# Stores of converted weight tiles issued by GpSimd instead of the sync engine

## The chip, the cores and the metric

The kernel runs on one NeuronCore of one Trainium2 chip. The metric is the device time of one execution in microseconds (us), taken as the median of several runs. Engine names in the text: PE is TensorE, DVE is VectorE, ACT is ScalarE, POOL is GpSimd, SP is the sync engine, whose queue issues transfers and computes nothing. "Issued by" an engine means that the instruction that starts a transfer stands in that engine's instruction stream and waits there for its conditions.

## The reference

Three layers follow one another: attention over a window of 64 positions (batch 4, 8 heads, 576 positions, head size 64), a gated feed-forward layer (512 to 1536 to 512) and a second one (512 to 2048 to 512), over 2304 tokens.

```python
scores = scale * np.matmul(q, k.transpose(0, 1, 3, 2))
mask = (rel >= 0) & (rel < 64)                  # rel: query position - key position
attn = softmax(np.where(mask, scores, -1e9))
x = np.matmul(attn, v)                          # [2304 tokens, 512]
g = x @ w_gate
x = (g * (1.0 / (1.0 + np.exp(-g))) * (x @ w_val)) @ w_out
h = x @ w_in
out = (h * np.clip(h + 3.0, 0.0, 6.0) / 6.0) @ w_out2
```

All weights arrive as 64-bit numbers and are made into pairs of 32-bit numbers on the chip.

## The kernel before, in words

**Weights.** The 68 raw weight tiles lie in DRAM as 128 x 512 numbers of 64 bits. The generator `w_ops` (called through `pump`) converts them, a few instructions at each call: ACT makes a float of the high word (L129) and scales the low word in place (L134), DVE clips, shifts and merges (L148, L151, L186, L192), ACT writes the rounded half `t[:, 0]` (L183) and DVE the remainder `t[:, 1]` (L199). The result is a tile of 128 x 1024 float32, a high and a low part. The 36 tiles of the first feed-forward layer stay in SBUF and are used there; 26 of them are also stored to the DRAM tensors `w1d` by `save_w` (L291), since their space is reused later and they are loaded again for the last blocks. The tiles of the second layer (32 raw ones and 16 sums of them, 48 in all) are written to staging tiles `ws` and stored to `w2d` at once (L205). A staging tile `ws` and a raw tile share the same five buffers (tag "raw"), so that a raw load (L107) can take a buffer only when the store of the `ws` tile that was in it has landed.

**Attention and the first layer.** After a first block of attention (0 to about 46 us), the first layer runs in 512-token blocks 0, 1 and 2, each in 12 steps. A step multiplies by the gate and value weights (L542 to L544), forms the product u, and adds the previous step's u times the output weights to four accumulators (L592 to L594). Between them stand the pieces of one attention group: scores (`scores`, L390), softmax on DVE and ACT, transposes (L452), the copy of the transposed tile out of PSUM (`evac_t`, L460, tile pt), the product with v (`values`, L471) and its copy (`store_x`). The loads of the next group, qk (L374, L377) and v (L382), are issued from SP, as are the raw weights. Step n calls `pump` three times, and from step 6 on it calls `save_w` once.

**Order.** Each engine works through its instructions in one fixed order. In the first block and from block 2 on the order is that of the code (`manual_schedule`). In blocks 0 and 1 a scheduler that models the engines and queues in time chooses the order of every engine's instructions, so a transfer that is issued by another engine can move instructions of all of them.

**Later stages.** The last 768 tokens of the first layer run in a form with fewer products (`wide_chunk`, about 396 to 520 us), and the second layer (`unit`, to the end) in two passes of 8 units, with the weights loaded from `w2d`.

Of the kernel before, what the change touches and what calls it, by code (L numbers as in the profile page):

```python
# [69 lines left out]
def attention_two_ffn(ctx: ExitStack, tc, qk, qq, v, w, out):  # L70
    nc = tc.nc
# [37 lines left out]
    def load_ahead(n):  # L109

        while len(w_loaded) <= n + (4 if len(w_loaded) < NW1 else 3):
            w_loaded.append(len(w_loaded))
            w_load(w_loaded[-1])

    def w_ops():

        held, words = {}, {}

        def begin(n):
            held[n] = cv.tile([128, 512], F32, tag="wf", name="wf", bufs=4)
            if raw_of[n] is not None:
                raw = w_raw.pop(raw_of[n])
                both = raw.bitcast(U32).rearrange("p (n t) -> p n t", t=2)
                words[n] = both[:, :, 0], both[:, :, 1]
                nc.scalar.activation(held[n], words[n][1].bitcast(F32), AF.Abs)  # L129

        def begin_low(n):
            if n in words:
                low = words[n][0]
                nc.scalar.activation(low.bitcast(I32), low, AF.Copy, scale=2.0 ** -29)  # L134

        begin(0)
        yield
        begin_low(0)
        yield
        for n in range(NV + 2):  # L140
            raw_n = raw_of[n] if n < NV else None
            new, sums, old = raw_n is not None, n < NV and raw_n is None, n >= 2
            if n < NV:
                f = held[n]
            if new:
                low, high = words.pop(n)
                u = f.bitcast(U32)
                nc.vector.tensor_scalar(f, f, F64_LOW, F64_HIGH, op0=ALU.max, op1=ALU.min)  # L148
                yield
            if new:  # L150
                nc.vector.tensor_scalar(  # L151
                    u, u, 3, 0x3FFFFFFF, op0=ALU.logical_shift_left, op1=ALU.bitwise_and
                )
                yield
            if sums:
                s0, s1 = f[:, 0:256], f[:, 256:512]
                if raw_of[n - 1] is not None:
                    fa, fb = held[n - 2], held[n - 1]
                    nc.vector.tensor_tensor(out=s0, in0=fb[:, 0:256], in1=fb[:, 256:512], op=ALU.add)
                    yield  # L160
                    nc.vector.tensor_tensor(out=s1, in0=s0, in1=fa[:, 0:256], op=ALU.subtract)
                    yield
                else:
                    fa, fb, fs = keep
                    nc.vector.tensor_tensor(
                        out=s0, in0=fa[:, 0:256], in1=fb[:, 0:256], op=ALU.subtract
                    )
                    yield
                    nc.vector.tensor_tensor(
                        out=s1, in0=fa[:, 256:512], in1=fs[:, 256:512], op=ALU.subtract  # L170
                    )
                    yield
            if n + 1 < NV:
                begin(n + 1)
                yield
            if old:
                if n - 2 < NW1:
                    pool = wp if n - 2 in ring else wq
                    t = pool.tile([128, 2, 512], F32R, tag="w", name="wt")
                else:  # L180
                    t = cv.tile([128, 2, 512], F32R, tag="raw", name="ws", bufs=5)
                o_f = held.pop(n - 2)
                nc.scalar.copy(t[:, 0, :], o_f)  # L183
                yield
            if new:
                nc.vector.scalar_tensor_tensor(  # L186
                    out=u, in0=high, scalar=0xC0000000, in1=u,
                    op0=ALU.bitwise_and, op1=ALU.bitwise_or,
                )
                yield  # L190
                i = f.bitcast(I32)
                nc.vector.tensor_tensor(out=i, in0=i, in1=low.bitcast(I32), op=ALU.add)  # L192
                load_ahead(raw_n)
                yield
            if n + 1 < NV:
                begin_low(n + 1)
                yield
            if old:
                nc.vector.tensor_tensor(  # L199
                    out=t[:, 1, :], in0=o_f, in1=t[:, 0, :].bitcast(F32), op=ALU.subtract  # L200
                )
                if n - 2 < NW1:
                    w_tile[n - 2] = t
                else:
                    nc.sync.dma_start(  # L205
                        out=w2_d[n - 2 - NW1],
                        in_=t.rearrange("p a n -> p (a n)").bitcast(F32),
                    )
                yield
            if sums and raw_of[n - 1] is not None:  # L210
                keep = fa, fb, f

    w_iter = w_ops()

    def pump(k):
# [72 lines left out]
    stream += [(load_w, ("w1o", c), w1_d[3 * c + 2]) for c in range(NC1)]  # L288

    def save_w(n):  # L290
        nc.sync.dma_start(  # L291
            out=w1_d[n], in_=w_tile[n].rearrange("p a n -> p (a n)").bitcast(F32)
        )

# [715 lines left out]
    with ExitStack() as fixed:  # L1010
# [10 lines left out]
        for n, (t, c) in enumerate(steps1):  # L1021
# [50 lines left out]
            if n >= SAVE_FROM and saves:  # L1072
                save_w(saves.pop(0))
# [144 lines left out]
```

## Time and profile before

| What | Value |
|---|---|
| Median of 3 runs (lowest, highest) | 920.91 us (919.66, 922.62) |
| Profiled execution | 920.93 us |
| Its span, first to last instruction | 919.1 us |
| PE busy | 891.6 us (97%), 5088 matmuls |
| DVE busy | 701.7 us (76%) |
| ACT busy | 418.1 us (45%) |
| POOL busy | 2.7 us, 14 instructions |
| DMA packets on the queue q1, SP's | 206.47 MB, 64.6% of 16 engines' time |

Busy time is the time that instructions of the engine were running; register work, waiting and the issuing of transfers do not count. PE's matmuls overlap, and their ends are modelled, so that the starts of neighbouring matmuls say more than their lengths. A row of waits names an instruction that stood still, what released it, how long in total, how many times, and the longest. A row of a transfer is its issue; when its bytes have arrived is its landing.

### The profile page before, as it was taken

What the parts mean: (1) busy time and instruction counts of PE and PEld (TensorE: products, weight loads), DVE (VectorE), ACT (ScalarE), POOL (GpSimd) and SP (SyncE); (2) the same over time, 40 slices, a digit from 0 to 9 for tenths busy, and PEclk for the clock granted to TensorE, in tenths of its full rate; (3) what the DMA queues carried; (4) which work ended last, traced back from release to release, by engine and by line L of the source; (5) the groups of instructions that cost most, each with busy time, mean ns of one, the idle gap of its engine ahead of it and who ended that gap; (6) DMA issues with size and microseconds to landing.
All of it is one profiled execution on the core that took longest, in us unless ns stands there. A gap on an engine that the chain in (4) does not pass through costs nothing.

```text
span 919.1 us, 14495 instructions
## 1 busy us (share of the span) xinstructions
PE 891.6 (97%) x5088; PEld 779.9 (85%) x5088; DVE 701.7 (76%) x1629; ACT 418.1 (45%) x994; POOL 2.7 (0%) x14
## 2 busy tenths in 40 slices
PE   5699999999999999999999999999999999999998
PEld 4487788887777778899999999898989898989896
DVE  7899999988887788698888667667666767565654
ACT  7788987665776766344444432222132222211111
POOL 1000000000000000000000000000000000000000
PEclk9799999999999999999999999999999999999999
DMA  8467997787785978315545479765477565485601
GB/s 325 134 196 237 354 352 258 245 296 273 260 307 171 333 279 296 132 60 194 181 146 168 178 303 359 251 217 192 161 293 294 194 207 203 169 311 198 215 24 69
DMA packets 67608, 207.52 MB, mean 226 GB/s; under 512 B 7248, under 2 KB 14416, under 8 KB 67152
## 3 DMA queue, kind: packets, MB, share of 16 engines
q1 hardware_dynamic: 67392, 206.47, 64.6%
q8 instruction: 40, 0.66, 0.3%
q14 instruction: 32, 0.26, 0.1%
q10 hardware_dynamic: 144, 0.13, 0.0%
HBM read 157.16 MB, written 49.41 MB: 225 GB/s over the span
## 4 chain that ended last, share of the span: by engine, by line
PE 65%; DVE 1%; ACT 1%; issue 0%; ACTq 0%; DVEq 0%
PE acc L891 5%; PE acc L892 5%; PE acc L890 5%; PE v L849 3%; PE v L851 3%; PE v L850 3%; PE g L849 3%; PE g L851 3%; PE g L850 3%; PE acc L593 2%; PE acc L594 2%; PE acc L592 2%; PE d L892 1%; PE c L892 1%; PE d L890 1%; PE c L890 1%
## 5 line engine op out<-in xcount | busy, mean ns | idle before, releaser
L870 ACT CAST gh<-g 128x384 fp32r<-128x384 f32 x96 | 49.3, 514 | 195.8 <-DVE g L861 165.2
L872 DVE TENSOR_TENSOR gl<-g,gh 128x384 fp32r<-128x384 f32 x96 | 53.3, 556 | 45.3 <-ACT gh L870 45.2
L593 PE MATMUL acc<-ul,wt 128*128 128x512 f32 (+1 forms) x216 | 81.6, 378 | 0.5 <-DVE ul L570 0.5
L594 PE MATMUL acc<-uh,wt 128*128 128x512 f32 (+1 forms) x216 | 80.4, 372 | 0.0
L892 PE MATMUL acc<-wt,gl 128*128 128x512 f32 x192 | 75.2, 391 | 0.0
L891 PE MATMUL acc<-wt,gh 128*128 128x512 f32 x192 | 75.1, 391 | 0.0
L890 PE MATMUL acc<-wt,gh 128*128 128x512 f32 x192 | 74.7, 389 | 0.0
L592 PE MATMUL acc<-uh,wt 128*128 128x512 f32 (+1 forms) x216 | 73.3, 373 | 0.2 <-ACT uh L565 0.2
L542 PE MATMUL g<-xh,wt 128*128 128x512 f32 x144 | 59.8, 415 | 3.3 <-ACT xh L331 2.8
L429 ACT ACTIVATE y<-y,s 128x128 f32<-128x128 f32 x144 | 56.2, 393 | 12.2 <-DVE s L423 11.9
L134 ACT ACTIVATE raw<-raw 128x512 int32<-128x512 uint32 x68 | 46.0, 677 | 30.9 <-DMA raw<-w_t 30.7
L542 PE MATMUL v<-xh,wt 128*128 128x512 f32 x144 | 57.3, 398 | 0.5 <-DVE u L585 0.4
L543 PE MATMUL g<-xl,wt 128*128 128x512 f32 x144 | 57.5, 399 | 0.2 <-DVE xl L332 0.2
L849 PE MATMUL v<-xh,wt 128*128 128x384 f32 x168 | 56.7, 338 | 0.4 <-ACT q L936 0.4
L544 PE MATMUL g<-xh,wt 128*128 128x512 f32 x144 | 57.1, 396 | 0.0
L849 PE MATMUL g<-xh,wt 128*128 128x384 f32 x168 | 56.6, 337 | 0.0
L544 PE MATMUL v<-xh,wt 128*128 128x512 f32 x144 | 56.5, 393 | 0.0
L851 PE MATMUL v<-xh,wt 128*128 128x384 f32 x168 | 56.4, 336 | 0.0
L851 PE MATMUL g<-xh,wt 128*128 128x384 f32 x168 | 56.4, 336 | 0.0
L850 PE MATMUL v<-xl,wt 128*128 128x384 f32 x168 | 56.3, 335 | 0.0
L850 PE MATMUL g<-xl,wt 128*128 128x384 f32 x168 | 56.3, 335 | 0.0
L543 PE MATMUL v<-xl,wt 128*128 128x512 f32 x144 | 56.2, 390 | 0.0
(214 smaller groups left out, 2274.1 us busy)
## 6 DMA issues: line engine op xcount, KB each, us to landing
wt<-w2d SPq DMA_DIRECT2D x144, 512.0 KB, 4.9
raw<-w_t SPq DMA_DIRECT2D x68, 512.0 KB, 5.0
w2d<-ws SPq DMA_DIRECT2D x48, 512.0 KB, 4.6
wt<-w1d SPq DMA_DIRECT2D x33, 512.0 KB, 4.4
w1d<-wt SPq DMA_DIRECT2D x26, 512.0 KB, 5.3
v<-v_t SPq DMA_DIRECT2D x36, 256.0 KB, 4.5
qk<-qk_t SPq DMA_DIRECT2D x21, 416.0 KB, 5.1
x_out<-ob SPq DMA_DIRECT2D x17, 256.0 KB, 2.1
```

Source lines behind the costliest of these rows:

```text
L542: nc.tensor.matmul(dst, wt[:, 0, col], hi, start=kc == 0, stop=False)
L543: nc.tensor.matmul(dst, wt[:, 0, col], lo, start=False, stop=False)
L544: nc.tensor.matmul(dst, wt[:, 1, col], hi, start=False, stop=kc == KC - 1)
L592: nc.tensor.matmul(a, wt[:, 0, col], hi, start=c == 0, stop=False)
L593: nc.tensor.matmul(a, wt[:, 0, col], lo, start=False, stop=False)
L594: nc.tensor.matmul(a, wt[:, 1, col], hi, start=False, stop=c == NC1 - 1)
L849: nc.tensor.matmul(dst, wt[:, 0, col], hi[:, k, :], start=k == 0, stop=False)
L850: nc.tensor.matmul(dst, wt[:, 0, col], lo[:, k, :], start=False, stop=False)
L851: nc.tensor.matmul(dst, wt[:, 1, col], hi[:, k, :], start=False, stop=k == 1)
L890: nc.tensor.matmul(a, hi[:, row], wt[:, 0, :], start=begin, stop=False)
L891: nc.tensor.matmul(a, hi[:, row], wt[:, 1, :], start=False, stop=False)
L892: nc.tensor.matmul(a, lo[:, row], wt[:, 0, :], start=False, stop=end)
```

## The change

Two calls change the engine that issues them. The store of a `ws` tile (L205) and `save_w` (L291) go from `nc.sync` to `nc.gpsimd`; what they transfer and when they are called stays as it was.

```diff
@@ w_ops
                 if n - 2 < NW1:
                     w_tile[n - 2] = t
                 else:
-                    nc.sync.dma_start(
+                    nc.gpsimd.dma_start(
                         out=w2_d[n - 2 - NW1],
                         in_=t.rearrange("p a n -> p (a n)").bitcast(F32),
                     )
@@ save_w
     def save_w(n):
-        nc.sync.dma_start(
+        nc.gpsimd.dma_start(
             out=w1_d[n], in_=w_tile[n].rearrange("p a n -> p (a n)").bitcast(F32)
         )
```

SP's order before, at the end of block 1 and the beginning of block 2 (xsd is attention output on its way through DRAM, x2d the first layer's output):

```order
L374 DMA qk<-qq_t 128x576
L107 DMA raw<-w_t 128x512
L205 DMA w2d_146<-ws 128x1024
L382 DMA v<-v_t 128x512
L493 DMA xsd<-xg 128x256
L107 DMA raw<-w_t 128x512
L205 DMA w2d_147<-ws 128x1024
L605 DMA x2d_77<-xr 128x2048
L382 DMA v<-v_t 128x512
```

SP's order now, at the same place:

```order
L382 DMA v<-v_t 128x512
L493 DMA xsd<-xg 128x256
L374 DMA qk<-qq_t 128x576
L107 DMA raw<-w_t 128x512 x2
L605 DMA x2d_77<-xr 128x2048
L382 DMA v<-v_t 128x512
L374 DMA qk<-qq_t 128x576
```

The stores of converted tiles have left SP. Of the two v loads in these rows, the first stood behind the store of w2d_146 before; now it is the first row, ahead of the qk and raw loads that it followed (the row in front of it is a qk load). POOL's order now, at the same place:

```order
L205 DMA w2d_146<-ws 128x1024
L205 DMA w2d_147<-ws 128x1024
L291 DMA w1d_115<-wt 128x1024
L205 DMA w2d_148<-ws 128x1024
L205 DMA w2d_149<-ws 128x1024
L291 DMA w1d_116<-wt 128x1024
```

These are the same stores in the same sequence as on SP before; between the mask instructions at the start and the end of the program POOL's order holds 74 stores and nothing else.

PE's order before, at the start of a step near the end of block 0 (y_1558 is a group's softmax output, d_1655 its transpose in PSUM, pt_1665 the copy of that in SBUF):

```order
L390 MATMUL c_1660<-qk_1542 128x128 x4
L542 MATMUL g_1668<-xh_620,wt_1568 128x512
L543 MATMUL g_1668<-xl_621,wt_1568 128x512
L452 MATMUL d_1655<-ident_167,y_1558 128x128 x2
L542 MATMUL v_1722<-xh_620,wt_1614 128x512
L543 MATMUL v_1722<-xl_621,wt_1614 128x512
L452 MATMUL d_1655<-ident_167,y_1558 128x128 x2
L544 MATMUL g_1668<-xh_620,wt_1568 128x512
```

PE's order now, at the same step:

```order
L452 MATMUL d_1655<-ident_167,y_1558 128x128 x4
L542 MATMUL g_1668<-xh_620,wt_1568 128x512
L543 MATMUL g_1668<-xl_621,wt_1568 128x512
L471 MATMUL c_1710<-pt_1665,v_1598 64x64 x7
L544 MATMUL g_1668<-xh_620,wt_1568 128x512
L542 MATMUL g_1668<-xh_624,wt_1568 128x512
```

The transposes stand together now, and the product with pt_1665 (L471, seven of its eight matmuls; the eighth follows ten gate matmuls later) has moved up to two gate matmuls behind them. Before, 24 matmuls of 512 columns stood between the last transposes and this product.

## Rows read from the trace of the kernel before

**Rows 1.** Windows: stretch, then us busy (x instructions), clock, DMA share, GB/s.

```profile
46.00:391.00 345.00, 339.91 (x2061) 274.90 (x2060) 300.29 (x789) 241.01 (x614) 0.00 (x0) 1.00 0.77 266
...
92.00:138.00 46.00, 45.57 (x274) 37.19 (x273) 44.65 (x119) 41.24 (x106) 0.00 (x0) 1.00 0.97 353
```

**Rows 2.** Waits of PE, 46 to 391 us: us in total, times, longest.

```profile
PE c L390 <- DMA qk<-qk_t: 1.4, 2, 0.9
PE c L471 <- DMA v<-v_t: 0.8, 1, 0.8
PE d L452 <- ACT y L441: 0.5, 1, 0.5
...
PE v L452 <- DVE u L585: 0.2, 1, 0.2
```

**Rows 3.** Waits of SP's queue, 46 to 391 us.

```profile
SPq L107 <- DMA w2d<-ws: 42.5, 15, 5.9
...
SPq L205 <- DVE ws L199: 28.0, 18, 4.7
...
SPq L291 <- DVE wt L199: 15.3, 10, 2.7
```

**Rows 4.** Tile ws: ns min/median/max, first and last start; landing in us.

```profile
L205 SPq DMA_DIRECT2D w2d<-ws x48: 319/326/2087, 160.6 to 373.2; - x48
...
DMA to landing us min/median/max: 2.6/4.6/7.5
```

**Rows 5.** Tensor w1d: its stores, in the same columns.

```profile
L291 SPq DMA_DIRECT2D w1d<-wt x26: 326/327/1832, 84.5 to 366.3; - x26
```

**Rows 6.** Timeline of SP: start us, us, engine, line, transfer.

```profile
200.05 0.40 SPq L205 DMA_DIRECT2D w2d<-ws  x1
200.54 0.44 SPq L377 DMA_DIRECT2D qk<-qk_t  x1
...
283.04 0.38 SPq L107 DMA_DIRECT2D raw<-w_t  x1
288.18 0.33 SPq L205 DMA_DIRECT2D w2d<-ws  x1
288.94 0.33 SPq L382 DMA_DIRECT2D v<-v_t  x1
```

**Rows 7.** Timeline of PE around one values group.

```profile
203.39 0.39 PE L543 MATMUL v<-xl,wt 128*128 128x512 f32 x1
203.62 0.39 PE L544 MATMUL v<-xh,wt 128*128 128x512 f32 x1
203.94 0.69 PE L471 MATMUL d<-pt,v 128*64 128x64 f32 x16
204.55 0.50 PE L592 MATMUL acc<-uh,wt 128*128 128x512 f32 x1
204.89 0.39 PE L593 MATMUL acc<-ul,wt 128*128 128x512 f32 x1
```

**Rows 8.** Waits of PE, whole span.

```profile
PE acc L471 <- ACT pt L460: 2.8, 3, 1.2
```

**Rows 9.** Groups by form: count, busy us, mean ns, idle before.

```profile
L460 ACT COPY pt<-d 128x512 f32<-128x512 f32 x14 | 8.1, 580 | 0.0
```

**Rows 10.** Waits of ACT, 46 to 391 us.

```profile
ACT raw L134 <- DMA raw<-w_t: 28.9, 28, 2.9
...
ACT ws L183 <- DMA w2d<-ws: 10.0, 7, 3.8
...
ACT wf L129 <- DMA raw<-w_t: 4.9, 1, 4.9
```

**Rows 11.** Groups by form, DVE alone.

```profile
L199 DVE TENSOR_TENSOR ws<-wf,ws 128x512 fp32r<-128x512 f32 x48 | 32.8, 685 | 5.4 <-ACT ws L183 5.3
...
L151 DVE TENSOR_SCALAR wf<-wf 128x512 uint32<-128x512 uint32 x68 | 28.2, 422 | 0.5
```

## Prediction

> **What bounds the kernel now.** I read the busy time by stage first, then what TensorE (PE) waited for, then what the sync engine's queue (SP) waited for, then the DMA issues and their landings. The stores in question are 48 of second-layer tiles and 26 of first-layer tiles, each 128 x 1024 x 4 bytes = 512 KB; all 74 are issued between 84.5 and 373.2 us [rows 4, 5], so the stage that counts is 46 to 391 us. There PE is busy 339.91 of 345.00 us [rows 1]: at most 5.1 us can be won from visible idle time. In 92 to 138 us three resources are near their limit together: PE 45.57 and VectorE (DVE) 44.65 of 46 us, DMA engines 0.97 busy at 353 GB/s [rows 1]. PE's own waits in the stage sum to 4.5 us in eight rows [rows 2]: 1.4 for qk loads, 0.8 for a v load, and six rows of 0.5 to 0.2 for ScalarE (ACT) and DVE. SP, in contrast, waits much: 28.0 us for DVE to finish tiles it stores at L205, 15.3 at L291, and 42.5 us at L107 for an earlier store to land so that its buffer can take a raw load [rows 3].
>
> **The change, part by part.**
>
> *Stores leave SP.* SP loses 74 issues. At about 0.40 us each (the store at 200.05 us [rows 6]) that is 30 us of its time, and the waits of L205 and L291 go with them. SP carries no arithmetic, so this is worth only what its loads gain by being earlier. Two places show it. A raw load is issued at 283.04; the store behind it waits for DVE until 288.18, and the v load behind the store starts only at 288.94 [rows 6]; PE's 0.8 us wait for v comes from this stretch. At 200.54 a qk load is issued 0.5 us behind a store [rows 6], on the same queue; PE waits for qk twice, 1.4 us in all [rows 2]. In the changed order that v load (the first row of SP's order now) stands behind a qk load and no store, so both kinds of wait should go: 1.4 + 0.8 = **2.2 us won**. Bounds: 0 (the bytes themselves are late) to 4.5 (all waits of [rows 2] go). What is late next on SP is its own condition at L107, the 42.5 us for landings [rows 3], which stays.
>
> *PE's order changes.* The scheduler lays out blocks 0 and 1 anew. Counted over the whole program's order, attention matmuls cut the rest of PE's work into 63 pieces before and 70 now. A break costs what the starts show: two matmuls of 512 columns start 0.23 us apart (203.39, 203.62); into an attention group it is 0.32 (to 203.94), and out of it 0.34 (204.55 to 204.89) [rows 7]. So 0.09 + 0.11 = 0.20 us, and 7 more pieces cost **1.4 us**. Bounds: 0 (they fall where PE would wait anyway) to 2.8 (twice that).
>
> *One short path in that order.* At the PE place shown above, `values` on tile pt_1665 now stands two matmuls (2 x 0.23 = 0.46 us) behind the transposes whose copy makes pt_1665; before, the distance was 24 matmuls. The copy at L460 takes 0.58 us on ACT, and where it was waited for in the first stage the longest wait was 1.2 us [rows 8, 9]. I take **0.5 us**, between 0 (ACT is ready and the matmuls' tail covers it) and 1.2.
>
> *Stores arrive on GpSimd (POOL).* Its 74 issues lie beside everything: after the mask work POOL has nothing else, and a store that waits there holds back only later stores. Who waits for a landed store is SP at L107 and ACT at L183, since raw loads and ws tiles share five buffers. What a POOL issue costs up to the landing the trace does not show: it has no DMA of POOL. The nearest rows are SP's own: 2.6 us at least, 4.6 median, 7.5 at most [rows 4]. So a store may land 2.0 us earlier or 2.9 later than the median; I take the median, **0**, because the 16 DMA engines and the bytes are the same, and the earlier issue (no queueing behind loads) offsets a slower one. To turn a later landing into time: in this stage ACT waited 28.9 + 10.0 + 4.9 = 43.8 us for these transfers [rows 10] while PE lost 5.1 us in all, so at most 0.12 us of PE per us of ACT. Bounds for 48 stores if each landing is passed on in full: 48 x 2.0 x 0.12 = 11.5 us won, which the 5.1 us of visible idle time caps, to 48 x 2.9 x 0.12 = 16.7 us lost.
>
> The Trainium skill speaks against the change here (SBUF — State Buffer, section "SBUF: two separate sides"): a DMA issued from GpSimd has its descriptors written by GpSimd's cores, and while DVE runs an operation that takes both port pairs they cannot be written, so the DMA starts late; it gives about 0.62 us alone and 3.1 us beside a copy. The trace has DVE operations that could be of that kind: L151 takes 422 ns for 512 columns where a two-input L199 takes 685 [rows 11]. By the page I would add to every landing; with its 2.5 us of difference on 48 stores my conversion would give 14 us, an estimate from the page's figures. No run here shows such a delay yet. The Trainium skill's page DMA: Bandwidth & Descriptors (section "Issuing engines are not separate DMA queues") says instead that the issuing engine changes only sequencer time, which by itself would leave the time as it is.
>
> **Sum.** The profiled execution took 920.93 us (span 919.1), the median of three is 920.91, so both serve as base. 920.9 - 2.2 + 1.4 + 0.5 + 0 = **920.6 us**. No change outside 46 to 391 us: before 46 us no such store is issued and the order is that of the code, and behind 391 us none is left.
>
> **Rivals.**
>
> *Faster: the stall-free stage.* With loads never behind stores, PE's waits for ACT and DVE shrink as well, because ACT's 43.8 us of waiting feeds them. All 4.5 us of [rows 2] go and the new breaks fall into former waits: 916.4 us. For it: SP's waits at L205 and L291. Against: the rows that name ACT or DVE in [rows 2] are of attention and of the product u, not of conversion; and DVE is at 97% in 92 to 138 us, so nothing upstream speeds up there.
>
> *Slower: stores land later.* Mechanism: a store issued by POOL lands about 1 us later than one by SP, inside the 2.9 us between SP's median and its slowest [rows 4]. The five shared buffers then come back later, the raw load at L107 too, ACT stands still in L134 or L183, the later instructions in ACT's order with it (exp, copies for PE), and PE waits. Price: 48 x 1 x 0.12 = 5.6 us on top of 920.6, 926.2 us; it decides from about half, 0.5 us per store. For it: 42.5 us of SP and 10.0 us of ACT already wait for just these landings [rows 3, 10]. Against: ACT is busy only 241.01 of 345 us [rows 1], so much of it is absorbed. The page SBUF — State Buffer of the Trainium skill, named above, gives a reason why such a delay could be there.
>
> *Nothing: the bytes are the limit.* In 92 to 138 us the DMA engines are 0.97 busy; whoever issues, loads and stores share them, the DMA waits stay or move, and PE's new order costs and wins alike: 920.9 us. The change would then take the stores off SP and not do what it says for the loads.
>
> **How the numbers follow.** What a measurement of this kernel can tell is about 0.3%, 2.8 us: faster means under 918.1, slower over 923.7. Chances: forecast 0.38, nothing 0.12, faster rival 0.20, slower rival 0.30. The forecast's own range is 917.5 to 923.5. Of the forecast I give 0.03 to each side beyond the limits, of the rivals 0.02 each back to the middle: faster 0.21, same 0.48, slower 0.31. The range has to take in most of both rivals: from 915.8 (920.9 less the 5.1 us of idle time) to 928 (the slower rival with 1.3 us per store: 920.6 + 48 x 1.3 x 0.12 = 928.1).
>
> **What would show it.** In the trace of the changed kernel: SP has no wait at L205 and L291, and PE's rows "L390 <- DMA qk" and "L471 <- DMA v" are gone or under 0.5 us together (first step). Starts around the split `values` group show 0.2 us per break and PE's wait for L460 is near 0.5 us (second and third). The landing of w2d stores has its median at 4 to 5 us (fourth); at 5.5 or more the slower rival holds, and ACT's waits for raw and ws are well over 43.8 us. PE busy in 46 to 391 us stays within 2 us of before. I am wrong if PE's idle time in that stage is over 8 us or under 2, or if anything before 46 us or behind 391 us moves by more than 1 us.

## Result and the profile after

The changed kernel takes 931.39 us (median of 4 runs, 929.25 to 932.25), the kernel before 920.99 in the same session: ratio 1.0105, interval [1.0085, 1.0126]. It is slower by about 10.4 us, above the whole predicted range. The profiled execution has a span of 930.5 us, 11.4 more than before.

The windows of the changed kernel, with the columns of [rows 1] (clock, DMA share and GB/s stand last):

```profile
46.00:391.00 345.00, 331.30 (x2012) 267.22 (x2011) 294.20 (x780) 238.58 (x609) 41.05 (x74) 1.00 0.78 266
92.00:138.00 46.00, 43.36 (x261) 34.80 (x260) 41.03 (x112) 38.71 (x102) 6.57 (x12) 1.00 0.95 334
138.00:299.00 161.00, 152.20 (x882) 123.54 (x882) 135.26 (x361) 105.23 (x269) 17.34 (x32) 0.99 0.73 250
```

PE idles 13.7 us in 46 to 391 us, where it idled 5.1 [rows 1]; it is less busy in 92 to 138 us as well (43.36 for 45.57). In 138 to 299 us it idles 8.8 us; before, it was 3.6:

```profile
138.00:299.00 161.00, 157.41 (x941) 127.55 (x940) 140.01 (x379) 107.09 (x283) 0.00 (x0) 1.00 0.75 259
```

The data rate over the stage is the same, 266 GB/s. The granted clock is not quite: the 0.99 in the row of the changed kernel comes from one drop. PE stands still for 1.74 us, runs again, and from 269.94 us the clock is at half, the level of 1.2 GHz, for 3.41 us. Matmuls of 512 columns then start 0.43 us apart, in place of 0.23 [rows 7]:

```profile
268.51 0.69 PE L471 MATMUL d<-pt,v 128*64 128x64 f32 x16 [1.74 <-ACT pt L460]
...
270.75 0.63 PE L592 MATMUL acc<-uh,wt 128*128 128x512 f32 x1
271.18 0.63 PE L593 MATMUL acc<-ul,wt 128*128 128x512 f32 x1
```

```profile
269.94:273.35 3.41, 3.41 (x10) 2.64 (x9) 3.31 (x10) 3.09 (x9) 1.07 (x2) 0.50 0.79 268
```

Eight matmuls of 512 columns were slowed in this way, so about 1.5 us of this execution is the drop, on top of the waiting. Two other stalls in the same trace, of 1.97 and 2.17 us, have no drop behind them. In the trace of before the clock is 1.00 from 46 to 391 us; in that of e1 (below) it drops once, for as long, behind a stall of 2.08 us. How many of the other executions have such a drop, the record doesn't show.

Where the time arises is seen by following ACT's 36 starts of L577, one for each of the first layer's steps, in both traces: the changed kernel is 0.3 us ahead at the first, 1.2 us late at the 6th, 7.1 at the 13th, 10.5 at the 24th, and still 10.3 at the 29th, in block 2. So nearly all of it is lost in blocks 0 and 1. In block 2, where 28 more stores (20 of them of w2 tiles) run on POOL but all engines follow the order of the code, little is: 11.0 at the last step.

PE's waits in the changed kernel (us in total, times, longest); compare [rows 2]:

```profile
PE d L471 <- ACT pt L460: 3.9, 2, 2.2
PE g L542 <- DVE u L578: 3.3, 3, 2.5
PE c L471 <- ACT pt L460: 2.0, 1, 2.0
PE v L452 <- DVE u L585: 1.7, 4, 0.9
PE d L471 <- DVE pt L460: 1.5, 1, 1.5
```

No row of PE in this stage names a DMA any more; the waits for qk and v are gone. In their place PE waits for ACT's and DVE's copies and products. Those engines are not slower: DVE is busy 702.3 us over the whole span (701.7 before). They are late. SP's and ACT's waits say for what:

```profile
SPq L107 <- DVE wf L192: 109.4, 34, 8.5
SPq L107 <- DMA w2d<-ws: 50.0, 11, 7.2
```

```profile
ACT raw L134 <- DMA raw<-w_t: 41.3, 27, 4.2
ACT ws L183 <- DMA w2d<-ws: 10.5, 9, 2.3
ACT wf L129 <- DMA raw<-w_t: 2.7, 1, 2.7
```

SP never waits at L205 or L291 now, but it waits at L107 instead, in front of raw loads that it reaches too early. Before, the first of these waits was shorter:

```profile
SPq L107 <- DVE wf L192: 34.3, 23, 4.5
```

ACT's three waits for transfers have grown from 43.8 us [rows 10] to 54.5. The stores themselves, in the columns of [rows 4]:

```profile
L205 POOL DMA_DIRECT2D w2d<-ws x48: 533/533/660, 165.5 to 384.6; - x48
...
DMA to landing us min/median/max: 2.9/4.7/7.7
```

The median landing, counted from the issue, hardly moved (4.6 before). That number misleads, as the experiments show. Two things escape it. An issue by POOL starts later behind the instruction that makes its tile: from the end of L199 to the start of the store the median is 0.03 us before and 0.40 now (0.41 in the kernels below), and POOL's smallest in any of these traces is 0.29. And the median runs over all 48 stores, 20 of them in block 2, where later landings cost little: from 299 to 391 us ACT waits 2.1 us for w2 stores (2.2 before) and no row of PE names a copy. Taken from the end of L199 to the landing, over the first 28 stores (issued before 290 us, in blocks 0 and 1), the mean is **4.75 us before and 5.69 after**. I call this made-to-landed below.

### The profile page after: what moved, and what is told of

The parts are those of the page before. It is cut to its first block, busy times and chain, and to the rows that moved or that the text cites. A ratio compares the mean times of both kernels' runs of the same rounds, so it can differ in the third digit from the quotient of the medians.

```text
span 930.5 us, 14535 instructions
## 1 busy us (share of the span) xinstructions
PE 894.4 (96%) x5088; PEld 781.5 (84%) x5088; DVE 702.3 (75%) x1629; ACT 419.3 (45%) x994; POOL 43.7 (5%) x88
## 4 chain that ended last, share of the span: by engine, by line
PE 62%; DVE 1%; DMA 1%; ACT 1%; issue 1%; DVEq 0%; ACTq 0%
PE acc L891 5%; PE acc L892 5%; PE acc L890 5%; PE v L849 3%; PE g L849 3%; PE v L851 3%; PE v L850 3%; PE g L851 3%; PE g L850 3%; PE acc L593 2%; PE acc L594 2%; PE acc L592 2%; PE d L892 1%; PE d L890 1%; PE c L890 1%; PE d L891 1%
## 5 line engine op out<-in xcount | busy, mean ns | idle before, releaser
L134 ACT ACTIVATE raw<-raw 128x512 int32<-128x512 uint32 x68 | 46.0, 676 | 43.2 <-DMA raw<-w_t 43.0
```

## Experiments

Two things changed together: the engine that issues the stores, and the order that the scheduler gave to PE, DVE, ACT and SP. The kernels below take them apart by imposing issue orders of one kernel on the other. The numbers of the traced instructions are the same in both kernels, so the edit is a table of them and a chain of edges that only fix the order:

```diff
+            read.update(range(NW1))
+    follow(tc, ORDERS, free)
...
+def follow(tc, orders, free):
+    """Each list: instruction numbers of one engine, in the order in which it is to issue them."""
...
+        for a, b in zip(names, names[1:]):
+            x, y = traced[f"I-{a}"], traced[f"I-{b}"]
+            if x.name not in free and y.name not in free:
+                continue
+            tc.add_manual_dep(y, x.name, info, reason="follow")
```

No run times a table on the kernel that it was read from. But the traces show that the tables do what they say: up to 410 us PE, DVE and ACT work through the sequence of before in e1 and through that of the changed kernel in e2. And they show that the edges put no waits in front of instructions: with the order of before imposed and the stores on sync (e8 below), PE, DVE and ACT have 919, 1556 and 1104 semaphore waits, the kernel before 919, 1557 and 1105. All ratios are to the kernel before, timed beside it (920.7 to 921.2 us).

**Order against engine.** Four kernels.

> Stores on GpSimd as in the changed kernel, but TensorE, VectorE, ScalarE and the loads on SP keep the order they had before (edges that only fix the order of issue). Order theory (the scheduler's new order in blocks 0 and 1 makes TensorE wait for attention pieces): 919 to 923 us, PE's waits on L460 and L578 in 46 to 391 us back under 1 us together. Issuer theory (a store issued by GpSimd disturbs loads, buffers or VectorE by itself): 928 to 933 us, PE idle in 46 to 391 us over 10 us.

> The mirror image: stores on SP as before, but TensorE, VectorE, ScalarE and the loads on SP in the changed kernel's order. Order theory: 928 to 935 us, with PE's waits on L460 and L578 of 8 us or more. Issuer theory: 919 to 923 us.

> Stores on GpSimd, only TensorE's order is that of before; the scheduler lays out VectorE, ScalarE and SP around it. If the loss lies in where TensorE's attention pieces stand: 918 to 923 us. If it lies in the order of conversion and softmax on VectorE and ScalarE, or in the issuer: 926 us or more.

> Stores on GpSimd, only VectorE's and ScalarE's orders are those of before; TensorE and SP are laid out around them. If the loss lies in VectorE's and ScalarE's order: 918 to 923 us. If it lies in TensorE's own order or in the issuer: 926 us or more.

Measured: e1 925.87 us, 1.0047 [1.0032, 1.0062]; e2 925.09, 1.0046 [1.0030, 1.0062]; e3 933.19, 1.0125 [1.0092, 1.0158]; e4 928.07, 1.0076 [1.0052, 1.0099]. Both theories miss with e1 and e2, and neither change alone is the cause: the new order without POOL costs 3.9 us by the medians (4.2 by the ratio), POOL without the new order 4.7 (4.4), both together 10.4, somewhat more than the sum. In e1 and e2 all engines are held. In e3 and e4 they are not, and there the scheduler laid out the free engines anew: DVE and ACT of e3, and PE of e4, have an order of neither kernel. So e3 and e4 don't tell which engine's order costs; their intervals both overlap that of the changed kernel.

In e1 every arithmetic instruction stands where it stood in the kernel before, so its trace can be laid beside the old one. ACT's timeline around 203 us, of before and then of e1 (start, duration, line; in brackets the idle time ahead and what ended it):

```profile
202.78 0.61 ACT L183 CAST ws<-wf 128x512 fp32r<-128x512 f32 x1
```

```profile
203.70 0.60 ACT L565 CAST uh<-u 128x512 fp32r<-128x512 f32 x1
206.13 0.62 ACT L183 CAST ws<-wf 128x512 fp32r<-128x512 f32 x1 [1.83 <-DMA w2d<-ws]
```

The same copy had no wait before and has 1.83 us now, for a w2 store. With e1's SP and POOL beside [rows 6]:

```profile
198.82 2.73 SPq L107 DMA_DIRECT2D raw<-w_t  x2
201.65 0.38 SPq L377 DMA_DIRECT2D qk<-qk_t  x1
```

```profile
200.95 0.53 POOL L205 DMA_DIRECT2D w2d<-ws  x1 [5.00 <-DVE ws L199]
202.15 0.65 POOL L205 DMA_DIRECT2D w2d<-ws  x1 [0.67 <-DVE ws L199]
```

Before, SP issued the second of these stores at 200.05 and the qk load behind it at 200.54 [rows 6]. In e1 that store goes out 0.5 us behind the qk load, and in its trace it takes 8.6 us to land, for 5.9 before. So a store on POOL is late twice: by itself, and because loads that stood behind it in one queue now go ahead of it.

The start times of the DMA packets, which the traces hold, tell both apart. Take the stores that are issued when all earlier transfers of their queue have landed, and that find no packet of a load moving 1.05 us later. Their first packet starts 0.82 us behind the issue on SP (two stores in the kernel before) and 1.10 to 1.22 us on POOL (five in e1). In the 14 stores of e1 that do find one moving it is 1.10 to 3.64 us, 1.58 at the median. By itself, then, a store on POOL is some 0.66 us later: 0.38 up to the issue and 0.28 behind it. Over the first 28 stores made-to-landed rises by little more, from 4.75 to 5.52 us. ACT's waits:

```profile
ACT raw L134 <- DMA raw<-w_t: 30.5, 27, 2.9
ACT ws L183 <- DMA w2d<-ws: 14.2, 12, 1.8
```

L183 waits 12 times for 14.2 us, in place of 7 for 10.0 [rows 10]. Laid beside before, ACT of e1 falls back by over 0.6 us at a time at eleven of its instructions in block 1; seven of them are L183, three L134.

**What about POOL costs.** Four kernels, all in the order of before.

```diff
@@ e5: only L205 on gpsimd; e6: only save_w on gpsimd; e7: all on gpsimd, and
+            if name in paced:
+                held = paced[name]
+            elif held:
+                tc.add_manual_dep(traced[name], held, sync, reason="pace")
@@ e8: all on sync, each w2 store behind a memset that waits for L199
+        nc.gpsimd.memset(pad[:, 0:HOLD], 0.0)
+        tc.add_manual_dep(extra[-1], made, sync, reason="hold")
```

> Only the 48 stores of w2 tiles (L205) are issued by GpSimd, the 26 of w1 tiles (L291) by sync; the order of the kernel before is imposed on TensorE, VectorE, ScalarE and the loads. All 74 on GpSimd in this order gave +0.47% (some 4.4 us). Theory A, late release: a store that GpSimd issues starts 0.41 us behind the subtraction L199 and not 0.03, so each of the five buffers shared by ws and raw comes free later and ScalarE's copy L183 waits; only w2 tiles share these buffers, so nearly all of it stays: 924.5 to 926.5. Theory B, pacing: sync, no longer held by stores, issues loads that compete or stand in each other's way; w1 stores held sync as well (15.3 of 43.3 us), so two thirds: 923 to 925. Theory C, a second queue takes its share of the bandwidth from the loads (19.0 against 21.6 GB/s per DMA engine): in proportion to the bytes, 48 of 74 stores, 923 to 924.5.

> The other half: only the 26 w1 stores are issued by GpSimd, the 48 w2 stores by sync, in the order of before. Theory A, late release: a w1 tile isn't overwritten until long after its store, so nothing is lost: 920 to 921.5, and sync's waits for wt at L291 (15.3 us) are gone, which may give up to 1 us back. Theory B, pacing: a third of 4.4 us, 922 to 923. Theory C, second queue: 26 of 74 stores, 922 to 923.

> All 74 stores on GpSimd, the order of before imposed, and in addition each load that stood behind a store in sync's queue now waits for the tile of that store (a dependency on the subtraction L199), so sync is held as it was in the kernel before. Theory B, pacing: the cost is gone, 920.5 to 922. Theory A, late release: the stores still start 0.4 us late, so nothing changes against the 925.9 of the unpaced one: 925 to 926.5. Theory C, second queue: the same, 925 to 926.5.

> The opposite: all stores stay on sync and its one queue, in the order of before, but each w2 store waits for a tiny GpSimd memset (128 x 8) that itself waits for the subtraction L199, so that it starts some 0.2 to 0.5 us later. Theory A, late release: the lateness alone costs it: with 0.4 us 924 to 926, in proportion with less or more. Theory B, pacing: sync is held longer, not less: 920 to 922. Theory C, second queue: there is none, 920.5 to 921.5; what sync's loads lose by standing 0.4 us longer behind the store is at most 1 us under B and C.

Measured: e5 925.50, 1.0055 [1.0037, 1.0074]; e6 923.95, 1.0045 [1.0028, 1.0063]; e7 928.75, 1.0100 [1.0074, 1.0126]; e8 925.50, 1.0054 [1.0036, 1.0072].

Pacing (B) falls with e7: SP held back again makes it worse, not better. It had named the wrong remedy: a load that waits for the same L199 as the store can still start ahead of it, since POOL needs 0.41 us more, and does so at 12 of the 48 stores. The second queue (C) misses all four ranges, and the two rates that it is built on don't show what it took them for (last section). Late release (A) has e5 inside its range, and misses e6 by 2.5 us and e7 by 2.3. e8 is inside the range for stores that start 0.4 us late, but they start only 0.22 us later than before, for which A, in proportion, asks 922.7 to 923.9. Made-to-landed over the first 28 stores agrees with A in e5 (5.66 us) and not in the others: e6 (4.83) and e8 (4.90) are hardly later than before, and e7 (5.53) is as late as e1 but 2.9 us slower. The costs of e5 and e6 don't add up to e1, either. In e6 something else happens. Its POOL queue, with no w2 stores between the w1 stores, lets them go in a burst (with idle time "issue", POOL waited for nothing shown):

```profile
158.61 1.60 POOL L291 DMA_DIRECT2D w1d<-wt  x3 [7.54 <-DVE wt L199]
162.54 0.53 POOL L291 DMA_DIRECT2D w1d<-wt  x1 [2.33 <-issue]
163.86 0.92 POOL L291 DMA_DIRECT2D w1d<-wt  x1 [0.78 <-issue]
167.44 0.53 POOL L291 DMA_DIRECT2D w1d<-wt  x1 [2.66 <-issue]
```

The qk load that SP issues at 164.88 us in the middle of it lands after 7.7 us, and the scores that need it are the largest gap in e6:

```profile
172.68 0.79 PE L390 MATMUL c<-qk 128*128 128x128 f32 x5 [2.19 <-DVE wf L186]
```

The releaser named there, a DVE instruction that ended at 172.65, has nothing to do with scores: the load landed at 172.54. In the kernel before the same load was issued at 164.92 and landed after 3.2 us.

e8 is only half understood. Its stores start at 0.25 us (median) behind L199, on one queue, and its made-to-landed over the first 28 is 4.90, 0.15 more than before; its profiled execution, the fastest of its six runs, idles PE only 5.26 us in the stage. The median of 925.50 says that something in it costs 4.6 us; the trace doesn't show what.

**Is it the landing?** The test that moves no instruction of the first layer: let the w2 stores land sooner.

```diff
-                        out=w2_d[n - 2 - NW1],
-                        in_=t.rearrange("p a n -> p (a n)").bitcast(F32),
+                        out=w2_d[n - 2 - NW1][:, 512:1024],
+                        in_=t[:, 1, :].bitcast(F32),
```

> All stores on GpSimd in the order of before, but each w2 store carries only the low half of its tile (256 of 512 KB), and the later loads of w2 read that half twice, so the output isn't the reference's. A full store landed 5.39 us after its tile was made (5.08 from sync); a half one should land 1 to 1.5 us sooner, more than the 0.3 us that GpSimd loses. Theory A, late landing: ScalarE's copies then find their buffers free, and this is no slower than its twin on sync: within 1 us of it, both 918 to 921.5. Theory E, something else that GpSimd's issue costs: the 4 us stay, 923 to 925.5 against 919 to 921 for the twin.

> The twin: the same halved w2 stores, issued by sync as in the kernel before, and in its order. Theory A, late landing: ScalarE's 10.0 us of waits for w2 stores shrink to under 4, and what TensorE idles in 46 to 391 us (5.1) shrinks by at most 2: 918 to 921. Theory E: the same, 919 to 921; the two theories differ in the twin on GpSimd.

Measured: POOL 917.89, 0.9973 [0.9955, 0.9991]; sync 917.95, 0.9974 [0.9963, 0.9985]. The whole difference between the engines is gone, as theory A said. (Both are just under its range, and ACT's waits for w2 stores in sync's twin, 7.9 us, are not under the 4 that it asked for.) POOL still starts each store 0.41 us late, still needs its 539 ns for an issue, still has a second queue. Made-to-landed over the first 28 is 4.28 us (POOL) and 3.73 (sync), both under the 4.75 of the kernel before. PE's idle time in the stage is 2.8 and 2.2 us:

```profile
46.00:391.00 345.00, 342.23 (x2078) 278.46 (x2077) 303.76 (x797) 243.04 (x616) 41.13 (x74) 1.00 0.68 229
...
ACT ws L183 <- DMA w2d<-ws: 4.3, 3, 1.8
...
DMA to landing us min/median/max: 2.3/3.3/6.5
```

```profile
46.00:391.00 345.00, 342.80 (x2080) 278.86 (x2079) 304.12 (x797) 242.37 (x616) 0.00 (x0) 1.00 0.69 229
...
ACT ws L183 <- DMA w2d<-ws: 7.9, 5, 4.2
...
DMA to landing us min/median/max: 2.0/3.4/6.7
```

The first fence is POOL's twin, the second sync's. What this does not tell is whether lateness or bytes are at work, since halving takes both away (DMA share 0.68 to 0.69 in place of 0.77).

**The order's half.** Two kernels on sync with one part of the new order each, and the halved stores in the new order.

> All stores on sync, only TensorE's order of after imposed (70 pieces in place of 63, the values two matmuls behind their transposes in one place), the other engines as in before. The whole order of after on sync gave +0.46% (4.2 us). Theory F, TensorE's order is what costs: 1.4 us for pieces and 0.5 to 2 us for the short place and its like: 922.5 to 925. Theory G, the order of VectorE and ScalarE costs: under 922. Theory H, each order is paid for only where it meets the other engines' old one: over 924 here and in the next kernel.

> All stores on sync, only the orders of VectorE and ScalarE of after imposed, TensorE and the loads as in before. Theory F, TensorE's order costs: 920 to 922. Theory G, the order of VectorE and ScalarE (conversion pieces put ahead of the copies pt and the activations that TensorE waits for) costs: 923.5 to 925.5. Theory H, mismatch: over 924, as in the kernel ahead of this.

> The halved w2 stores again (low half only, loads of w2 read it twice, so the output isn't the reference's), now on GpSimd in the order of after on every engine. In the order of before the halved stores came to 917.9 us on either engine. Theory A, late landing, taken further: the order, too, costs only because the five buffers that ws and raw share leave no slack, so with early landings after's order is nearly as good: 917.5 to 920. Theory K, the order costs by itself (pieces and copies that stand late in it), whatever the stores do: 4 us more than 917.9, 921 to 923.5.

> The same halved stores on sync, in the order of after. Late landing taken further: 917.5 to 920. The order by itself: 921 to 923.5. By either the twin on GpSimd is within 1 us of this; if GpSimd costs something that isn't the landing, the twin is slower by 3 us or more.

Measured: e11 923.98, 1.0043 [1.0028, 1.0059]; e12 925.61, 1.0050 [1.0034, 1.0066]; e13 922.10, 1.0019 [1.0006, 1.0032]; e14 919.91, 0.9998 [0.9985, 1.0010].

The expectations of e11 and e12 say that the other engines keep their order; the kernels don't do that, since only the named engines are held. In e12 PE fell into place as in the changed kernel (its sequence differs in a few matmuls), so it is nearly e2 again and repeats it (925.09). In e11 PE has the new order, and DVE and ACT have an order of neither kernel. So no kernel here has one engine in the new order and the others in the old, and theories F, G and H are not decided.

With halved stores the new order costs 2.0 us on sync (919.91 against 917.95) and 4.2 on POOL (922.10 against 917.89). So on sync about half of what the order costs goes with the whole stores, by their lateness or their bytes, and POOL costs 2.2 us under the new order even then: made-to-landed over the first 28 stores is 4.66 us there and 3.83 on sync, both no later than the 4.75 of before. Neither theory is the whole, and that something else about POOL costs time under the new order is not excluded.

What stays can be partly named. It is, first, the place that the prediction spoke of, the product with pt_1665 two gate matmuls behind its transposes. It in the changed kernel, and in e11:

```profile
131.16 0.62 PE L471 MATMUL c<-pt,v 128*64 128x64 f32 x13 [1.97 <-ACT pt L460]
```

```profile
130.47 0.65 PE L471 MATMUL c<-pt,v 128*64 128x64 f32 x14 [0.51 <-ACT pt L460]
```

The wait is 1.97 us; PE's order is the same in e11, but ACT's isn't, and there it is 0.51. ACT in the changed kernel shows why:

```profile
128.82 0.68 ACT L134 ACTIVATE raw<-raw 128x512 int32<-128x512 uint32 x1
129.38 0.40 ACT L429 ACTIVATE y<-y,s 128x128 f32<-128x128 f32 x1
...
129.77 0.39 ACT L429 ACTIVATE y<-y,s 128x128 f32<-128x128 f32 x1
...
130.16 0.39 ACT L429 ACTIVATE y<-y,s 128x128 f32<-128x128 f32 x1
...
130.54 0.57 ACT L460 COPY pt<-d 128x512 f32<-128x512 f32 x1
```

The transposes ended at 128.3 us. Between them and the copy stand three exponentials of the next group, 1.2 us. In the kernel before ACT made this copy at 130.33 us, but PE used it only at 134.85. A second case, ACT of the changed kernel around 238 us:

```profile
237.87 0.65 ACT L134 ACTIVATE raw<-raw 128x512 int32<-128x512 uint32 x1 [4.15 <-DMA raw<-w_t]
238.43 0.60 ACT L183 CAST ws<-wf 128x512 fp32r<-128x512 f32 x1
238.94 0.58 ACT L460 COPY pt<-d 128x512 f32<-128x512 f32 x1
```

The transposes ended at 233.1. The copy stands behind a conversion that waits 4.15 us for its raw load, and PE waits 2.17 us for it. That is how the two halves meet: a late transfer costs PE time where the order puts something that PE needs behind it.

**Four copies moved.** Order tables of after on all engines, with four numbers of the tables for ACT and DVE moved up; nothing else.

> The changed kernel (stores on GpSimd, its own order on all engines) with four of the copies pt (L460) moved up in their engine's order: on ScalarE pt_1665 ahead of three exponentials, pt_2680 ahead of two conversions ws and one of raw, pt_2898 ahead of one of raw; on VectorE pt_2566 ahead of a subtraction L199. In the trace of after TensorE waited 1.97, 2.17, 1.74 and 1.46 us for these four. Theory L, the place of the copies in the order is what these waits cost: about 5 to 6 of 931.4 us come back, 925 to 927.5. Theory M, the engines are late anyway because conversions wait for transfers, and TensorE meets the next late instruction instead: 929 to 931.5.

> The same moves with all stores on sync, in the order of after (925.1 us without the moves). There TensorE waited 0.94 and 1.29 us for pt_1665 and pt_2898, and less for the two others. Theory L: some 1.5 to 2.2 us come back, 922.5 to 924. Theory M: 924.5 to 925.5.

Measured: POOL 927.80, 1.0092 [1.0073, 1.0111] (the interval is wide: five runs, 927.16 to 931.24); sync 923.05, 1.0023 [1.0011, 1.0036]. On sync some 2 us come back (from 1.0046 to 1.0023), as the theory that blames the place of the copies says. With the stores on POOL the median misses that theory's range by 0.3 us; it is 3.6 us below that of the changed kernel, but the ratios, 1.0092 and 1.0105, have intervals that largely overlap, so a gain is not shown there. In the POOL version PE's waits for copies are down to 0.2 us, but the next late instruction takes some of their place:

```profile
PE g L542 <- DVE u L578: 4.2, 4, 1.6
PE d L452 <- ACT xr L483: 1.5, 1, 1.5
...
PE c L471 <- ACT pt L460: 0.2, 1, 0.2
```

**A store in two parts.** All bytes, in two stores of 256 KB, the high half without waiting for L199.

```diff
+                    nc.sync.dma_start(
+                        out=w2_d[n - 2 - NW1][:, 0:512], in_=t[:, 0, :].bitcast(F32)
+                    )
                     nc.sync.dma_start(
-                        out=w2_d[n - 2 - NW1],
+                        out=w2_d[n - 2 - NW1][:, 512:1024],
```

> A version that computes all: stores on sync, in the order of before, but each w2 tile goes out in two stores of 256 KB, the high half (which ScalarE's copy L183 makes) without waiting for the subtraction L199, the low half behind it. All bytes are still moved. Theory A: what frees the buffer is the landing of the low half, some 0.3 to 1 us sooner than that of the whole; 0.2 to 0.3 us later cost 4 us, so this gives some back: 918 to 920.5. If the bytes on their way set the landings, not their start: 920.5 to 922, with 48 more issues on sync.

> The same two stores for each w2 tile, both issued by GpSimd, in the order of before (925.9 with whole stores on GpSimd). Theory A: the low half starts 0.41 us late, or up to 0.5 us later still where GpSimd is busy issuing the high half, but is half as long, so most of the 4.4 us come back: 919 to 922.5. If the bytes on their way set the landings: 924.5 to 927.

Measured: sync 929.58, 1.0094 [1.0076, 1.0111]; POOL 927.05, 1.0072 [1.0056, 1.0089]. Neither is a version to keep. Both miss the ranges of late landing; POOL's time is just above the one for bytes on their way, sync's is beyond either. In the trace of the sync version ACT waits 14.2 us for w2 stores in 11 waits, and the median landing of these stores, each half as long, is 4.4 us, nearly that of the whole tiles (4.6). The buffer comes free with the low half, and over the first 28 tiles that lands 4.90 us behind L199, where the whole tile took 4.75. So splitting the store brings its end no sooner here; why it costs 8.8 us on sync, these runs don't show.

## Why the prediction was wrong

*Stores leave SP, 2.2 us won.* The mechanism was right: SP doesn't wait at L205 and L291, and PE's rows for qk and v are gone, in the changed kernel and in e1. The gain can't be seen in the time. The prediction took it that nothing would hold PE in place of these waits; what did was ACT and DVE, late in the order or held by transfers, and that cost more.

*Seven breaks, 1.4 us.* Not measured alone: no kernel has PE's new order beside the others' old ones, so no run shows this term.

*The short path, 0.5 us.* Mis-sized: 1.97 us, above my bound of 1.2. I read PE's order only and supposed that ACT would be ready, as in e11 it is, where 0.51 us were measured. In the changed order ACT does three exponentials first. Copies that stand late in ACT's and DVE's order are, with e18, about 2 of the 3.9 to 4.2 us that the order costs, and I priced one of them.

*POOL's landing, 0 us.* This step failed most, and with the mis-sized order it took the forecast along. I equated issue-to-landing for both engines, and by my own test (median 4 to 5 us) it even looks right at 4.7. The bytes are indeed the same, but three things are not: the start behind L199 (0.41 for 0.03 us) and of the first packet behind the issue (1.10 for 0.82), the place among the loads, and the stores that count. In e1 the stores of blocks 0 and 1 land 0.77 us later (5.52 for 4.75), and e1 is 4.4 to 4.7 us slower; with stores of half the bytes, which land early, the engine makes no difference in this order (e9, e10). That the lateness is what costs is argued from these two and from ACT's waits in e1, and e6, e7 and e8 don't follow it. My argument that the earlier issue would offset a slower one was the wrong way round: the loads became earlier, not the stores.

*The slower rival* had the mechanism: buffers back later, ACT still, PE waits. Its rate comes out too low: 28 x 0.77 x 0.12 = 2.6 us, where 4.4 to 4.7 were measured. The rate turns ACT's waits into PE's and leaves out what a stall brings with it, such as the 3.41 us at half clock in the profiled execution of e1. The rival missed, too, that the order would cost nearly as much again, 3.9 to 4.2 us against my 1.9 for breaks and short path, and that the two add.

*Two slips in the working* change nothing in this. 74 issues at the medians of [rows 4, 5], 0.33 us, are 24 us of SP's time and not 30, and 48 x 1 x 0.12 is 5.8 us and not 5.6.

*The rule of the Trainium skill* (SBUF — State Buffer, section "SBUF: two separate sides"), that a DMA from GpSimd starts late while DVE holds the port pairs, is not seen here at the 2.5 us that I used: with DVE busy 294.20 of 345 us the median landing is 4.7 us in the changed kernel and in e1, 5.0 in e5 and 4.9 in e7, against 4.6. Nor is it seen behind the single issue. Nine stores of e1 and the changed kernel found POOL's queue empty and no packet of a load moving; their first packets came 1.10 to 1.22 us behind the issue, and DVE ran L148 or L151 meanwhile in three of them (1.10, 1.22 and 1.22 us). The longer starts in these two traces, up to 4.26 us, are all of stores that found packets of loads moving. The other page, DMA: Bandwidth & Descriptors (section "Issuing engines are not separate DMA queues"), agrees with e9 and e10, where the engine makes no difference; it does not hold for the time of the whole program, since e1 differs by 0.47% in nothing but the issuing engine and what follows from it, and e13 from e14 by 2.2 us.

*What stays open.* The 3 us of e6, of which its largest gap shows 2.2, the 2.9 us that e7 adds to e1, and e8's 4.6 us, which its trace doesn't show. How much of the landing's cost is lateness and how much the bytes beside it, since e9 and e10 take away both. And the rest of the order's cost, about 2 us on sync with the copies moved. A sixth shared buffer would ask the question of slack directly; no run has one. No version that computes all is faster than the kernel before.

## What to carry to other kernels

Before a transfer is moved to another queue, look at who waits for its end, and measure from the instruction that makes the data to the landing, in the stage where someone waits, not the median from issue to landing over the program. One queue is also an order: a store that stood ahead of loads is overtaken by them when it goes to its own queue, and here the change of engine alone came to more than 4 us, with landings that were 0.77 us later on a ring of five shared buffers. And where a scheduler lays the program out anew, read the order of every engine in the chain, not only that of the engine that waits: the short distance on PE cost 0.5 us, three instructions on ACT made it 2.0.

## What was not expected of the hardware

With stores on a second queue, packets of the loads seem to move more slowly and those of the stores faster: in 160 to 280 us of e1 the loads' packets make 19.0 GB/s on a DMA engine and the stores' 25.1, where the one queue of before made 21.6 (bytes over the time that the packets took). But that one queue held loads and stores, and both queues of e1 together make 21.3. Packets of 4096 bytes, which raw loads and stores have in common, make 22.1 before and 21.8 over both queues of e1. So the split shows that in e1 the stores' packets are quicker than the loads'; that a second queue changed either is not shown. POOL's issue of such a store occupies it for 533 ns, SP's 326 (median).
